# A filter read straight into SBUF by SyncE's queue, and weight conversion steps placed anew, in the opening of a GFNet kernel

## The chip, the cores and the metric

One core of a Trainium2 chip. The metric is the device time of one execution in microseconds (us), the median over runs. PE is TensorE, PEld its weight load, DVE VectorE, ACT ScalarE, POOL GpSimd, SP SyncE; SP computes nothing here and issues transfers.

## The reference

```python
def _attn_ref(x, filt_r, filt_i):            # x: 8 x 3008 x 256, filters: 1505 x 256
    X = np.fft.rfft(x, axis=1)
    F = (filt_r + 1j * filt_i)[None, :, :]
    y = np.fft.irfft(X * F, n=x.shape[1], axis=1)
    return y.astype(np.float32)

def _moe_ref(x, w_in, w_out, alpha=1.0):     # x: 24064 x 256, w_in: 256 x 2048, w_out: 2048 x 256
    h = x @ w_in
    g = np.where(h > 0.0, h, alpha * (np.exp(np.minimum(h, 0.0)) - 1.0))
    return (g @ w_out).astype(np.float32)
```

Each of eight batches of 3008 tokens is mixed along the sequence (real Fourier transform, product with a complex filter, inverse), and the mixed tokens go through a feed-forward layer with an ELU between its two matrices. All is float32, but `moe_w_in` and `moe_w_out` arrive as float64.

## The kernel before

*Mixing.* 3008 = 47 x 64, so the transform is two steps of matmuls with a table of twiddles between (64 points, then 47). The frequencies are done in groups: eight groups g for the first batch. Its inverse goes the same way back, through the DRAM buffers `z` and `yd`.

*Feed-forward.* `w_in` and `w_out` are cut into four quarters q, and each product of two-by-two blocks is done with seven products in place of eight (a Strassen form), which needs sums of blocks of the weights (`w_sums`) and of the data (`n_sums`). An item (b, m, q) is one batch, one sixth of its tokens and one quarter; `up_steps` makes its first matrix product and the ELU, `down_steps` the second. 192 items follow each other; an item's place in this order is called a *quad* (number i). The order of all instructions is written out by hand (`tc.manual_schedule()`, L817), and what belongs to the mixing of the next batch is put into the quads by a dictionary `plan`: `at(quad, place, fn, ...)`, where places 2 and 3 lie within the first half of a quad, 0 in its middle and 1 at its end. Quad i of batch b's mixing counts from t = (b - 1) x 24. The mixing of batch 1 thus runs under the feed-forward of batch 0.

*The opening* (L820 to L936) has the mixing of batch 0, with functions of its own. `x_load_first` reads x in six chunks (SP); `a_first` makes the first transform of a chunk, 16 matmuls, evicted by ACT; `t_first` transposes; `b_first(g)` makes the second transform of a group (PE), then `products` (L336 to L339) multiplies with the filter `ff[:, g]` in four DVE operations of 128 x 512; `bi_first` starts the inverse; `y_write_first` writes it to `yd`. `y_read` and `n_unit` read it back and end the inverse for a sixth m; they are called two quads ahead of the item (m = 0 in the opening).

*The filter* must stand in `ff` with 48 rows for each of two halves (a = 0 in partitions 0 to 47, a = 1 in 64 to 111): 24 even rows, which are frequencies 64 apart counted upwards, and 23 (or 24) odd ones counted downwards. `f_arrange` (L785) first copies both filters into that order in a DRAM tile `fd` (L183), by transfers of POOL's queue whose 23 odd rows go as 16 and 7 (L794); `f_read_first` (L319) then reads a group as one transfer for each half. For batches 1 to 7 `f_pairs` (L804) builds another order `fp` from `fd`, DRAM to DRAM, in four calls (c, u) at the end of quads 1 to 4 in SP's queue; `f_read` reads it with POOL's.

*The weights.* Float64 is made float32 on the chip, in sixteen pieces k of 128 x 512 (four per quarter: two of `w_in`, two of `w_out`). `w_fetch(k)` loads a piece (0.5 MB), `w_split` takes mantissa and exponent bits of the high word (two DVE operations), `w_float` turns low word, mantissa and exponent into floats (four ACT operations), `w_join` sets the sign, adds the mantissa's parts and multiplies by the power of two (three or four DVE operations), `w_sums` makes the block sums of two pieces (four operations). These are spread over the opening and the first quads. Their buffers are borrowed from other work (`fbufs`, `t2`, the x chunks, `zq`, `rq`, ...).

*Queues.* Each engine issues its own transfers in program order. A transfer of SP's queue takes one of eight completion semaphores in turn, so its issue waits until the transfer eight before it has landed. `raw(src, row, ap)` builds an access pattern by hand: a list of [step, count], outermost first.

Of the kernel before, what the change touches and what calls it, by code (L numbers as in the profile page):

```python
# [11 lines left out]
FP32 = mybir.dt.float32  # L12
# [121 lines left out]
def kernel(  # L134
# [48 lines left out]
    fd = fdp.tile([NG, 2, 48, 2, 2, D], FP32, name="fd")  # L183
# [135 lines left out]
    def f_read_first(g, t):  # L319
        for a, r in enumerate((LO, HI)):  # L320
            nc.gpsimd.dma_start(t[r].rearrange("p c u d -> p (c u d)"), fd[g, a].rearrange("q c u d -> q (c u d)"))
# [391 lines left out]
    def w_fetch(k, queue=nc.gpsimd):  # L713
        q, j = divmod(k, 4)

        if k in (3, 4, 14, 15):
            wd = t2[:, k % 11 - 3].rearrange("p u d -> p (u d)")
        elif k == 10:
            wd = t1p.tile([P, XC, D], FP32, tag="t1", name="wd").rearrange("p u d -> p (u d)")
        elif k in (6, 7, 8, 9):  # L720
            wd = xp.tile([P, 2, 2, D], FP32, tag="xc", name="wd").rearrange("p k u d -> p (k u d)")
        else:
            wd = fbufs[{5: 0, 11: 0, 12: 1, 13: 2}.get(k, k)].rearrange("p c u d -> p (c u d)")
        wd = wds[k] = wd.bitcast(U32).rearrange("p (a w) -> p a w", w=2)
        if j < 2:
            srcs = [moe_w_in.bitcast(U32)[ts(j, P), ts(q, 1024)]]
        else:
            srcs = [moe_w_out.bitcast(U32)[ts(4 * q + 2 * (j - 2) + i, P), :] for i in range(2)]
        for i, s in enumerate(srcs):
            n = 512 // len(srcs)  # L730
            queue.dma_start(wd[:, ts(i, n), :].rearrange("p a w -> p (a w)"), s)
# [6 lines left out]
    def w_split(k):  # L738
        m, e, f, l = wts[k] = wtmp[{9: 2, 10: 1, 11: 0, 12: 3, 13: 4, 15: 5}.get(k, k % 2)]
# [4 lines left out]
    def w_float(k, *parts):  # L744
        m, e, f, l = wts[k]
        ef = e.bitcast(FP32)
        steps = ((l, wds[k][:, :, 0], AXT.Identity, 2.0 ** -52, 0.0), (f, m, AXT.Identity, 2.0 ** -20, 1.0),
                 (ef, e, AXT.Relu, -8.0, edges[:, 0:1]), (e, ef, AXT.Relu, -1.0, edges[:, 1:2]))
        for i in parts or range(4):
            o, x, func, scale, bias = steps[i]  # L750
            nc.scalar.activation(out=o, in_=x, func=func, scale=scale, bias=bias)

    def w_join(k, parts=(0, 1)):
        q, j = divmod(k, 4)
        m, e, f, l = wts[k]
        if 0 in parts:
            nc.vector.scalar_tensor_tensor(out=e, in0=wds.pop(k)[:, :, 1], scalar=0x80000000, in1=e,
                                           op0=ALU.bitwise_and, op1=ALU.bitwise_or)
            nc.vector.tensor_tensor(out=f, in0=f, in1=l, op=ALU.add)
        if 1 not in parts:  # L760
            return
        e = e.bitcast(FP32)
        if j < 2:
            f, e = (t.rearrange("p (a j c) -> p a j c", a=2, j=2) for t in (f, e))
            dst = w_in[q][:, 2 * j:2 * j + 2, :, :].rearrange("p j a c -> p a j c")
            nc.vector.tensor_tensor(out=dst, in0=f, in1=e, op=ALU.mult)
        else:
# [3 lines left out]
            for i in range(2):  # L771
                nc.vector.tensor_tensor(out=dst[:, i], in0=f[:, i], in1=e[:, i], op=ALU.mult)
        if j % 2 == 1 and k < 7:
            w_sums(k)
# [10 lines left out]
    def f_arrange():  # L785

        for c, src in enumerate((filt_r, filt_i)):
            for a in range(2):
                nc.gpsimd.dma_start(fd[:, a, 0:48:2, c, :, :].rearrange("g q u d -> q g (u d)"),
                                    raw(src, 2 * a, [[64 * D, 24], [4 * D, NG], [1, 2 * D]]))  # L790
                for u in range(2):
                    g0 = 1 if a == u == 0 else 0
                    for j, n in ((0, 16), (16, 7)):
                        nc.gpsimd.dma_start(fd[g0:NG, a, 1 + 2 * j:2 * (j + n):2, c, u, :].rearrange("g q d -> q g d"),  # L794
                                            raw(src, 64 * (j + 1) - 4 * g0 - 2 * a - u,
                                                [[64 * D, n], [-4 * D, NG - g0], [1, D]]))

                g0 = 0 if a else 1
                nc.gpsimd.dma_start(fd[g0:NG, a, 47, c, :, :].rearrange("g u d -> g (u d)"),
                                    raw(src, 4, [[2 * D, NG - g0], [1, 2 * D]]))  # L800
            nc.gpsimd.dma_start(fd[0, 0, 1:48:2, c, 0, :], raw(src, 32, [[64 * D, 24], [1, D]]))
            nc.gpsimd.dma_start(fd[0, 0, 47:48, c, 1, :], raw(src, 4, [[D, 1], [1, D]]))

    def f_pairs(c, u):  # L804

        src = fd.rearrange("g a q c u d -> (g a) q c u d")[:, :, c, u, :]
        dst = fp.rearrange("g (a u) k c h d -> (g a) u k c h d", u=2)[:, u, :, c, :, :]
        nc.sync.dma_start(dst[:, :, 0, :], src[:, 0:48:2, :])
        g = 1 - u
        nc.sync.dma_start(dst[g:, 1:24, 1, :], src[g:, 1:46:2, :])  # L810
        nc.sync.dma_start(dst[g:, 0, 1, :], nil_d[g:])
        if u == 0:
            nc.sync.dma_start(dst[0, :, 1, :], src[0, 1:48:2, :])

    with tc.manual_schedule():


        with tc.tile_pool(name="boot", bufs=1) as bp:
# [10 lines left out]

            for z in zt[0] + zt[1]:  # L830
                nc.gpsimd.memset(z.rearrange("p (k r) -> p k r", r=ROWS)[:, :, 48:64], 0.0)
            for k in (1, 2, 3):
                w_fetch(k)
            f_arrange()
            w_fetch(0, nc.sync)
            for c in range(NXC):
                x_place_first(c)
            for c in range(3):
                x_load_first(c)
            w_fetch(4, nc.sync)  # L840
            nc.scalar.memzero(ff[:, 0:NG // 2])
            nc.vector.memset(ff[:, NG // 2:NG], 0.0)
            def places(m, e, c):
                wtmp.append((m.bitcast(U32), e.bitcast(U32), c[:, 0], c[:, 1]))

            def flat(t):
                return t.rearrange("p a b -> p (a b)")

            places(*(kp.tile([P, 512], FP32, tag=t, name=n) for t, n in (("k0", "wm"), ("k1", "we"))),
                   kp.tile([P, 2, 512], FP32, tag="c", name="wfl"))  # L850
            places(*(flat(sdp.tile([P, 2, D], FP32, tag="sd", name=n)) for n in ("wm", "we")),
                   t1p.tile([P, XC, D], FP32, tag="t1", name="wfl").rearrange("p (a b) d -> p a (b d)", a=2))
            for i, v in enumerate((1151.0 * 2 ** 23, 255.0 * 2 ** 23)):
                nc.vector.memset(edges[:, i:i + 1], v)

            def step(k):
                w_split(k)
                w_float(k)
                if k > 0:
                    w_join(k - 1)  # L860

            for k in range(3):
                step(k)
            w_fetch(5, nc.sync)
            for c in (3, 4):
                x_load_first(c)
            a_first(0)
            w_fetch(6, nc.sync)
            x_load_first(5)
            nc.sync.dma_start(once, once_d)  # L870
            nc.sync.dma_start(gs, gs_d)
            step(3)
            for c in (1, 2):
                a_first(c)
                w_fetch(c + 6, nc.sync)
            step(4)
            a_first(3)
            w_fetch(9, nc.sync)
            step(5)
            step(6)  # L880
            for c in (4, 5):
                a_first(c)
            tn_read(0, 0)
            for g in range(NG):
                f_read_first(g, ff[:, g])
            w_fetch(10)
            c = t1p.tile([P, XC, D], FP32, tag="t1", name="wfl").rearrange("p (a b) d -> p a (b d)", a=2)
            places(c[:, 0], flat(tnp.tile([P, 4, P], FP32, tag="tn", name="we")), c)
            for t in (zq, rq):
                t = t.rearrange("p a u d -> p a (u d)")  # L890
                places(t[:, 0], t[:, 1], t[:, 2:4])
            t = t3f.rearrange("p a (b u) d -> p (a b) (u d)", u=2)
            places(t[:, 0], t[:, 1], t[:, 2:4])
            w_split(7)
            w_join(6)
            w_split(8)
            floats = {0: (7, 0, 1), 1: (7, 2, 3), 2: (8, 0, 1), 3: (8, 2, 3), 4: (9, 0, 1), 5: (9, 2, 3), 6: (10, 0, 1)}
            for g in range(4):
                t_first(g)
            for g in range(NG + 2):  # L900
# [9 lines left out]
                if g in floats:  # L910
                    w_float(*floats[g])
                if g == 1:
                    w_split(9)
                if g == 2:
                    w_join(7)
                    w_sums(7, nc.gpsimd)
                if g == 5:
                    w_split(10)
                if 3 <= g < 6:
                    w_fetch(g + 8, nc.sync)  # L920
            y_read(0, 0, slice(0, K2 - 4), slice(K2 - 4, K2))
            for k in (14, 15):
                w_fetch(k, nc.sync)
            w_float(10, 2, 3)
            w_join(8)
            for k in (11, 12, 13):
                w_split(k)
                w_float(k)
            w_join(9)
            w_sums(9)  # L930
            w_join(10)
            w_join(11)
# [22 lines left out]
        for quad, place, fn, *a in ((0, 0, w_split, 14), (0, 0, w_sums, 11), (1, 2, w_join, 12), (1, 2, w_split, 15), (1, 2, w_float, 14, 0, 1),  # L955
                                    (1, 3, w_float, 14, 2, 3), (2, 2, w_float, 15, 0, 1), (2, 3, w_float, 15, 2, 3),
# [120 lines left out]
```

## Time and profile before

| what | value |
|---|---|
| median of 3 runs | 2561.13 us (2560.88 to 2561.38) |
| profiled execution, its own time | 2561.57 us |
| its span | 2559.8 us |
| PE busy | 2519.9 us, 98% of the span |
| PEld busy | 2162.6 us, 84% |
| DVE busy | 2067.4 us, 81% |
| ACT busy | 1543.9 us, 60% |
| POOL busy | 159.5 us, 6% |
| SP's queue (q1) | 214308 packets, 166.86 MB |
| POOL's queue (q0) | 14000 packets, 30.44 MB |
| first matmul of the feed-forward (L574) | 88.01 us |

The span is the time from the first to the last instruction that the profiler saw, and the time of the same execution is 1.8 us longer. A share of busy time is an average over the span: the opening and the feed-forward have different limits, and are read apart below. In a chain of waits each row is a piece of the path that ended last: when it starts, how long it takes, and which engine, tile and line it is. In rows by stretch, (x17) is the number of instructions that fell into it, and a DMA share of 1.00 means that all sixteen DMA engines of the core were busy all the time (it can come out a little above).

### The profile page before, as it was taken

Reading aid. Unit: us, or ns where it says so; the run is one execution under the profiler, and the core shown is the slowest. Engines: PE = TensorE matmul, PEld = TensorE weight load, DVE = VectorE, ACT = ScalarE, POOL = GpSimd, SP = SyncE. Lnnn points to the kernel's source line nnn. Section 1 sums busy time; section 2 is a strip of 40 time slices with the busy share of each in tenths; the row PEclk is TensorE's granted clock in tenths of the full one; section 3 lists DMA queues with packets and bytes.
Section 4 is the critical chain, followed back from the end, with each engine's and each line's share of the span. In section 5 each row is a group of like instructions: output and inputs, shape, how many; then the busy total and the mean of one; then the engine's idle time right before and its main releaser. Section 6 shows DMA issues by size and latency. Waiting matters only on the chain.

```text
span 2559.8 us, 43989 instructions
## 1 busy us (share of the span) xinstructions
PE 2519.9 (98%) x16682; PEld 2162.6 (84%) x16682; DVE 2067.4 (81%) x3578; ACT 1543.9 (60%) x2715; POOL 159.5 (6%) x315
## 2 busy tenths in 40 slices
PE   6999999999999999999999999999999999999998
PEld 4788889888898888988889888888889888898887
DVE  6978887788878888688877888778897788876766
ACT  6766556655566555666566656566655655555554
POOL 5001000000000000000000000000100010000000
PEclk9999999999999999999999999999999999999999
DMA  9662213523233221433225231353213322110010
GB/s 282 183 186 67 59 44 78 131 63 71 48 99 98 69 66 40 127 81 74 51 51 143 66 77 36 77 123 80 66 38 84 87 63 63 38 44 18 20 27 17
DMA packets 229879, 200.56 MB, mean 78 GB/s; under 512 B 129398, under 2 KB 201990, under 8 KB 229668
## 3 DMA queue, kind: packets, MB, share of 16 engines
q1 hardware_dynamic: 214308, 166.86, 26.6%
q0 software_dynamic: 14000, 30.44, 4.2%
q8 instruction: 131, 2.15, 0.4%
q14 instruction: 80, 0.66, 0.1%
q10 hardware_dynamic: 1360, 0.46, 0.1%
HBM read 125.80 MB, written 78.12 MB: 80 GB/s over the span
## 4 chain that ended last, share of the span: by engine, by line
PE 96%; DMA 2%; DVE 1%; ACT 0%; issue 0%; SPq 0%; DVEq 0%; ACTq 0%
PE po L656 45%; PE phs L574 25%; PE phd L574 13%; PE pha L574 6%; PE psn L526 2%; PE psa L236 2%; PE pf L387 1%; PE pv L459 1%; DMA xc<-in_x_dram 1%; PE po L332 0%; DMA x<-in_x_dram 0%; PE po L298 0%; PE psr L332 0%; PE psa L279 0%; DVE g L582 0%
## 5 line engine op out<-in xcount | busy, mean ns | idle before, releaser
L656 PE MATMUL po<-g,wo 128*128 128x256 f32 (+1 forms) x5376 | 1317.7, 377 | 0.0
L656 PEld LDWEIGHTS po<-g,wo 128*128 128x128 f32 x5376 | 1010.7, 190 | 165.8 <-issue 49.6
L585 ACT ACTIVATE g<-phs 128x512 f32<-128x512 f32 (+1 forms) x576 | 338.8, 588 | 736.7 <-PE phs L574 735.3
L592 ACT ACTIVATE e<-e 128x512 f32<-128x512 f32 (+1 forms) x768 | 477.2, 621 | 24.4
L596 DVE SCALAR_TENSOR_TENSOR g<-e,g 128x512 f32<-128x512 f32 (+1 forms) x576 | 387.5, 673 | 13.7 <-ACT e L592 13.3
L582 DVE TENSOR_TENSOR g<-phd,g 128x512 f32<-128x512 f32 (+1 forms) x384 | 259.0, 674 | 165.1 <-ACT e L592 107.6
L574 PE MATMUL phs<-y,wi 128*128 128x256 f32 (+1 forms) x1536 | 387.6, 375 | 1.3 <-ACT y L509 1.3
L574 PE MATMUL phd<-y,wi 128*128 128x256 f32 (+1 forms) x1504 | 380.3, 375 | 0.0
L591 ACT ACTIVATE e<-g 128x512 f32<-128x512 f32 (+1 forms) x576 | 354.4, 615 | 34.3 <-DVE g L582 26.8
L574 PEld LDWEIGHTS phs<-y,wi 128*128 128x128 f32 x1536 | 291.4, 190 | 34.7 <-ACT y L509 1.5
L574 PEld LDWEIGHTS phd<-y,wi 128*128 128x128 f32 x1504 | 284.8, 190 | 35.1 <-DVE g L582 2.7
L596 DVE SCALAR_TENSOR_TENSOR g<-e,phs 128x512 f32<-128x512 f32 (+1 forms) x192 | 129.9, 677 | 115.2 <-ACT e L592 115.2
L574 PE MATMUL phs<-yt,wi 128*128 128x256 f32 (+1 forms) x768 | 193.9, 375 | 0.9 <-ACT g L585 0.9
L574 PE MATMUL phs<-yb,wi 128*128 128x256 f32 (+1 forms) x768 | 193.8, 375 | 0.6 <-ACT g L585 0.6
L574 PE MATMUL pha<-yb,wi 128*128 128x256 f32 (+1 forms) x736 | 185.9, 375 | 0.0
L591 ACT ACTIVATE e<-phs 128x512 f32<-128x512 f32 (+1 forms) x192 | 112.3, 585 | 111.9 <-PE phs L574 111.8
L582 DVE TENSOR_TENSOR g<-pha,g 128x512 f32<-128x512 f32 (+1 forms) x192 | 129.5, 674 | 44.8 <-PE pha L574 44.8
L574 PEld LDWEIGHTS phs<-yt,wi 128*128 128x128 f32 x768 | 145.7, 190 | 18.0 <-ACT g L585 1.5
L574 PEld LDWEIGHTS phs<-yb,wi 128*128 128x128 f32 x768 | 144.0, 190 | 19.3 <-ACT g L585 1.0
L326 POOL DMA_DIRECT2D fall<-fp x224 | 110.0, 499 | 721.9 <-DVE r L432 697.1
L574 PEld LDWEIGHTS pha<-yb,wi 128*128 128x128 f32 x736 | 139.8, 190 | 16.1
L633 DVE TENSOR_TENSOR g<-g,g 128x512 f32<-128x512 f32 (+1 forms) x192 | 130.7, 681 | 6.7
(166 smaller groups left out, 2063.3 us busy)
## 6 DMA issues: line engine op xcount, KB each, us to landing
yd<-t SPq DMA_DIRECT2D x127, 192.0 KB
t<-yd SPq DMA_DIRECT2D x92, 256.0 KB
z<-t SPq DMA_DIRECT2D x84, 256.0 KB
fall<-fp POOLq DMA_DIRECT2D x224, 96.0 KB, 2.9
t<-z SPq DMA_DIRECT2D x224, 96.0 KB
out_dram<-o SPq DMA_DIRECT2D x632, 32.0 KB
xc<-in_x_dram SPq DMA_DIRECT2D x84, 128.0 KB
xc<-in_x_dram SPq DMA_DIRECT2D x161, 64.0 KB
```

The lines of the kernel that those rows point to most:

```text
L236: nc.tensor.matmul(p[o:o + 64, u, :], w[r, u, o:o + 64], src[r, u, :], start=True, stop=True)
L326: nc.gpsimd.dma_start(t[32 * a:32 * a + 24].rearrange("p c u d -> p (c u d)"), fp[g, a].rearrange("q c u d -> q (c u d)"))
L387: nc.tensor.matmul(pf[p][1][32 * a:32 * a + 32, js, :], fb[r, v, :], t2[r, js, a, :], start=True, stop=True, tile_position=(32 * p, 32 * a))
L526: nc.tensor.matmul(p[ts(c, 64), dh, ts(q, 64)], t[r, i - 4 * m, ds(dh * P + 64 * c, 64)], w[r, i - 4 * m, :], start=True, stop=True)
L574: nc.tensor.matmul(ps[:, a, 0:h], w_in[q][:, COMBO[n], a, :], y[n], start=start and a == 0, stop=True, skip_group_check=True)
L582: nc.vector.tensor_tensor(out=g[o], in0=i0, in1=i1, op=ALU.add)
L585: nc.scalar.activation(out=g[o], in_=i0, func=AXT.Copy)
L591: nc.scalar.activation(out=e, in_=src, func=AXT.Relu, scale=-1.0)
L592: nc.scalar.activation(out=e, in_=e, func=AXT.Exp, scale=-1.0)
L596: nc.vector.scalar_tensor_tensor(out=g[n], in0=es[n], scalar=1.0, in1=src, op0=ALU.subtract, op1=ALU.max)
L633: nc.vector.tensor_tensor(out=b12, in0=b22, in1=b12, op=ALU.subtract)
L656: nc.tensor.matmul(po[i][:, u, 0:h], w_out[q][:, COMBO[n], a, :], g[n][:, a, :], start=q == 0 and a == 0 and n in (1, 3, 6, 4), stop=True, ...
```

## The change

In the opening the DRAM copy `fd` and `f_arrange` go. `f_read_first(g, n)` reads n groups at once from `filt_r` and `filt_i` into `ff`, by SP's queue: for each filter and half one transfer of the 24 even rows (2 KB runs for each group) and up to two of the 23 odd rows (1 KB runs), 36 transfers in three calls for group 0, groups 1 to 3 and groups 4 to 7. They stand behind the last chunk of x and two tables (`once`, `gs`), ahead of weights 4 to 7, the first inverse's twiddles (`tn_read`) and weight 8. Weights 0 to 2 are loaded by POOL's queue at the start, all others by SP's. `f_pairs` reads the filters themselves; the transfer of the 23 odd rows now has these 23 outermost on both sides (before: the 15 or 16 half-groups).

The conversion: `w_float` has three ACT steps, and a fourth for k > 9; the sign is a function `w_sign`; `w_join` scales and adds the mantissa in one DVE operation for k up to 9, adds on POOL for k > 9, and multiplies on POOL for k from 4; all `w_sums` are on POOL. Splits and floats stand one per group in groups 3 to 7 of the opening (after `products`), and those of pieces 11 to 15 in quads 0 to 2, two pieces each, with sign, join and sums. Buffers of the pieces are assigned anew.

```diff
-    fd = fdp.tile([NG, 2, 48, 2, 2, D], FP32, name="fd")
...
-    def f_read_first(g, t):
-        for a, r in enumerate((LO, HI)):
-            nc.gpsimd.dma_start(t[r].rearrange("p c u d -> p (c u d)"), fd[g, a].rearrange("q c u d -> q (c u d)"))
+    def f_read_first(g, n):
+
+        t = ff[:, g:g + n]
+        for c, src in enumerate((filt_r, filt_i)):
+            for a in range(2):
+                o = 64 * a
+                k = 4 * g + 2 * a
+                nc.sync.dma_start(t[o:o + 48:2, :, c].rearrange("q g u d -> q g (u d)"),
+                                  raw(src, k, [[64 * D, 24], [4 * D, n], [1, 2 * D]]))
+                for u in range(2):
+                    e = 1 if k + u == 0 else 0
+                    if n > e:
+                        nc.sync.dma_start(t[o + 1:o + 47:2, e:n, c, u],
+                                          raw(src, 64 - 4 * e - k - u, [[64 * D, 23], [-4 * D, n - e], [1, D]]))
+            if g == 0:
+                nc.sync.dma_start(t[1:48:2, 0, c, 0], raw(src, 32, [[64 * D, 24], [1, D]]))
...
-    def w_fetch(k, queue=nc.gpsimd):
+    def w_fetch(k, queue=nc.sync):
...
     def w_split(k):
-        m, e, f, l = wts[k] = wtmp[{9: 2, 10: 1, 11: 0, 12: 3, 13: 4, 15: 5}.get(k, k % 2)]
+        m, e = wts[k] = wtmp[k % 3 if k < 10 else (1, 3, 4, 0)[k % 4 - 2]]
...
-    def w_float(k, *parts):
-        m, e, f, l = wts[k]
-        ef = e.bitcast(FP32)
-        steps = ((l, wds[k][:, :, 0], AXT.Identity, 2.0 ** -52, 0.0), (f, m, AXT.Identity, 2.0 ** -20, 1.0),
-                 (ef, e, AXT.Relu, -8.0, edges[:, 0:1]), (e, ef, AXT.Relu, -1.0, edges[:, 1:2]))
+    def w_float(k):
+
+        m, e = wts[k]
+        ef, l = e.bitcast(FP32), wds[k][:, :, 0]
+        steps = [(l.bitcast(FP32), l, AXT.Identity, 2.0 ** -52, 1.0),
+                 (ef, e, AXT.Relu, -8.0, edges[:, 0:1]), (e, ef, AXT.Relu, -1.0, edges[:, 1:2])]
+        if k > 9:
+            steps.append((m.bitcast(FP32), m, AXT.Copy, 2.0 ** -20, 0.0))
...
+    def w_sign(k):
+        m, e = wts[k]
+        nc.vector.scalar_tensor_tensor(out=e, in0=wds[k][:, :, 1], scalar=0x80000000, in1=e,
+                                       op0=ALU.bitwise_and, op1=ALU.bitwise_or)
+
+    def w_join(k):
         q, j = divmod(k, 4)
...
+        e, f, l = e.bitcast(FP32), m.bitcast(FP32), wds.pop(k)[:, :, 0].bitcast(FP32)
+        if k > 9:
+            nc.gpsimd.tensor_tensor(out=f, in0=f, in1=l, op=ALU.add)
+        else:
+            nc.vector.scalar_tensor_tensor(out=f, in0=m, scalar=2.0 ** -20, in1=l, op0=ALU.mult, op1=ALU.add)
+        engine = nc.vector if k < 4 else nc.gpsimd
...
-                nc.vector.tensor_tensor(out=dst[:, i], in0=f[:, i], in1=e[:, i], op=ALU.mult)
-        if j % 2 == 1 and k < 7:
-            w_sums(k)
+                engine.tensor_tensor(out=dst[:, i], in0=f[:, i], in1=e[:, i], op=ALU.mult)
...
-    def f_arrange():
...
     def f_pairs(c, u):
 
-        src = fd.rearrange("g a q c u d -> (g a) q c u d")[:, :, c, u, :]
+        src = (filt_r, filt_i)[c]
         dst = fp.rearrange("g (a u) k c h d -> (g a) u k c h d", u=2)[:, u, :, c, :, :]
-        nc.sync.dma_start(dst[:, :, 0, :], src[:, 0:48:2, :])
+        nc.sync.dma_start(dst[:, :, 0, :], raw(src, u, [[2 * D, 2 * NG], [64 * D, 24], [1, D]]))
         g = 1 - u
-        nc.sync.dma_start(dst[g:, 1:24, 1, :], src[g:, 1:46:2, :])
+        nc.sync.dma_start(dst[g:, 1:24, 1, :].rearrange("g k d -> k g d"),
+                          raw(src, 64 - 2 * g - u, [[64 * D, 23], [-2 * D, 2 * NG - g], [1, D]]))
...
+            for k in range(3):
+                w_fetch(k, nc.gpsimd)
...
+            step(0)
+            a_first(0)
+            w_fetch(3)
+            for c in (4, 5):
                 x_load_first(c)
...
             nc.sync.dma_start(once, once_d)
             nc.sync.dma_start(gs, gs_d)
+            for g, n in ((0, 1), (1, 3), (4, 4)):
+                f_read_first(g, n)
+            step(1)
+            a_first(1)
+            step(2)
+            a_first(2)
+            a_first(3)
             step(3)
...
             for c in (4, 5):
                 a_first(c)
+            for k in range(4, 8):
+                w_fetch(k)
             tn_read(0, 0)
-            for g in range(NG):
-                f_read_first(g, ff[:, g])
...
+            w_fetch(8)
+            w_sign(3)
+            w_join(3)
+            for k in (1, 3):
+                w_sums(k, nc.gpsimd)
...
+                if 3 <= g < 9:
+                    if g < 8:
+                        w_split(g + 1)
+                        w_float(g + 1)
+                    if g > 3:
+                        w_sign(g)
+                        w_join(g)
+                    if g == 7:
+                        for k in (5, 7):
+                            w_sums(k, nc.gpsimd)
+                if 4 <= g < 7:
+                    w_fetch(g + 5)
...
-            for k in (14, 15):
-                w_fetch(k, nc.sync)
...
+            for k in (12, 13, 14, 15):
+                w_fetch(k)
+            w_split(9)
+            w_float(9)
+            w_split(10)
+            w_float(10)
+            w_sign(9)
             w_join(9)
-            w_sums(9)
-            w_join(10)
-            w_join(11)
+            w_sums(9, nc.gpsimd)
...
+        for quad, place, fn, *a in ((0, 2, w_sign, 10), (0, 2, w_join, 10), (0, 2, w_split, 11), (0, 2, w_float, 11),
+                                    (0, 0, w_sign, 11), (0, 0, w_join, 11), (0, 0, w_sums, 11, nc.gpsimd),
+                                    (0, 0, w_split, 12), (0, 0, w_float, 12),
+                                    (1, 2, w_sign, 12), (1, 2, w_join, 12), (1, 2, w_split, 13), (1, 2, w_float, 13),
+                                    (1, 0, w_sign, 13), (1, 0, w_join, 13), (1, 0, w_sums, 13, nc.gpsimd),
+                                    (1, 0, w_split, 14), (1, 0, w_float, 14),
+                                    (2, 2, w_sign, 14), (2, 2, w_join, 14), (2, 2, w_split, 15), (2, 2, w_float, 15),
+                                    (2, 0, w_sign, 15), (2, 0, w_join, 15), (2, 0, w_sums, 15, nc.gpsimd)):
```

## The prediction

> **What bounds the kernel now.** I read the shares by engine first, then the chain of waits, then busy time in 20 us stretches. Chain of the whole span:
>
> ```profile
> PE 96%; DMA 2%; DVE 1%; ACT 0%; issue 0%; SPq 0%; DVEq 0%; ACTq 0%
> ```
>
> PE is full but for the opening, where the chain runs (start, length in us, what):
>
> ```profile
> 15.18 14.30 DMA xc<-in_x_dram
> 29.50 10.89 DMA x<-in_x_dram
> 40.53 3.63 PE psa L279 x16
> 48.28 0.36 PE psr L332
> 67.48 0.26 PE psi L332
> 74.47 0.60 DVE zq L339
> 85.07 1.71 ACT rq L751 x3
> 88.01 1.02 PE phs L574 x4
> ```
>
> So x's last piece lands at 40.39; the eight frequency groups run from 48.3 to 75.1 (PE sets their pace, 2.57 us a group: forward 0.95, back 1.72); then the weights' last steps, and the first FFN matmul at 88.01. Behind it (stretch, length, busy PE, PEld, DVE, ACT, POOL, then PE clock, DMA share, GB/s):
>
> ```profile
> 20.00:40.00 20.00, 12.11 (x64) 11.27 (x64) 9.15 (x20) 11.25 (x26) 8.72 (x16) 0.83 1.05 343
> 40.00:60.00 20.00, 19.01 (x144) 13.38 (x148) 15.52 (x31) 14.95 (x31) 9.56 (x18) 0.91 1.00 285
> 80.00:100.00 20.00, 15.73 (x74) 12.07 (x73) 16.70 (x36) 16.66 (x31) 0.00 (x0) 1.00 0.96 252
> 120.00:140.00 20.00, 19.39 (x144) 16.73 (x143) 18.68 (x36) 14.01 (x25) 0.52 (x1) 1.00 0.60 168
> ```
>
> DMA is saturated to 60 us; PE has gaps up to about 140 us, none later. Whatever the change does is thus seen in the opening, in the first quads, and where a late transfer makes a full PE wait.
>
> **How a transfer is shared out.** The row that decides this forecast is the DMA share while one kind of transfer runs alone: transfers of 16 rows (L810), of 64 (L310), of 24 (L316), of 24 again (L470):
>
> ```profile
> 105.50:106.00 0.50, 0.50 (x5) 0.50 (x4) 0.50 (x3) 0.42 (x1) 0.00 (x0) 1.00 1.07 330
> 157.00:157.75 0.75, 0.75 (x56) 0.75 (x60) 0.00 (x0) 0.60 (x1) 0.75 (x2) 1.00 0.93 290
> 163.75:164.10 0.35, 0.35 (x3) 0.32 (x2) 0.35 (x2) 0.35 (x1) 0.00 (x0) 1.00 0.76 199
> 219.50:222.00 2.50, 2.50 (x14) 2.19 (x13) 2.40 (x7) 0.60 (x1) 0.00 (x0) 1.00 0.70 143
> ```
>
> 16 and 64 rows fill the 16 engines, 24 rows keep 0.70 to 0.76 of them: 12, each with two rows. I read it as equal shares: as many engines as the largest number up to 16 that divides the outermost rows. The change makes transfers whose outermost dimension is 23 rows, a prime: one engine. Before has none: the 23 odd rows of a filter half are split 16 + 7 (L794), and the copy into pairs (L810) has 15 or 16 outermost. Price of a 1 KB row on one engine: 330 GB/s over 16 engines is 20.6 GB/s, 50 ns; 290 over 0.93 x 16 is 52 ns; 255 over 0.93 x 16 (0 to 20 us) 60 ns; 143 over 0.70 x 16 80 ns. I take 50, from the row with the same 1 KB runs; ends 46 (the median 1 KB packet of the trace) and 80.
>
> The Trainium skill, "DMA: Bandwidth & Descriptors", section "Why a DMA increments its semaphore by 16 and not by 1", states the same: the largest k up to 16 dividing the slowest dimension on both sides, with 127 partitions as an example of k = 1. The trace agrees at 24 rows; no run here shows a prime yet. It speaks against this change: by it 23 rows have a sixteenth of the bandwidth.
>
> **Part by part.**
>
> *x.* Ahead of x5 the old order has the copy into DRAM and weights 4 to 6, written and read (GpSimd's issues from 4.6 to 35.5 us). Now about 6.8 MB stand there (x, its tables, weights 0 to 3): at (255+343)/2 = 299 GB/s 22.8 us, plus some 2.5 to start: 25 instead of 40.4. The first group could then start at 34.5, not 48.3: 14 us gained.
>
> *Filter straight into SBUF.* Odd rows by size: group 0 6 x 23 = 138 KB, groups 1 to 3 8 x 69 = 552, 4 to 7 8 x 92 = 736; 1426 rows of 1 KB. The even ones (24 rows, 2 KB runs, 1.57 MB on 12 engines) put another 128 on the same engine. 1554 x 50 ns = 78 us, the first just before x's end: last landing near 102.5. Group 0 is there at 32, 1 to 3 at 62, 4 to 7 at 102. Transfers with few engines don't run at once either: each of SyncE's waits for its eighth predecessor, and they queue on the same engine anyhow.
>
> *What waits for it.* Weights 4 to 7, the twiddles of the first inverse and weight 8 stand behind all 36 in SyncE's queue: weight 4 at 103.6. On VectorE the split of weight 4 stands ahead of the products of group 4: these start at 104.3 (before: 49.4 + 4 x 2.57 + waits, near 64). Behind products 4 each group has on VectorE products 4 x 0.60 = 2.4, split 2 x 0.335, sign 0.6, join 0.65: 4.3 us, and thrice this and the last 2.4 is 15.3; the sign waits some 2 to 3 us for ScalarE's three float steps (0.57 each behind two evictions of 0.5 that come later): last product at about 122.5, 47.4 later than 75.07. From there to the first FFN matmul 12.94 us before; now weights 9 and 10 only (two splits, floats, one sign, join and four sums of 0.76 on GpSimd), and the last group's evictions, y's write and read: I keep 13. First FFN matmul 135.6: **+47.6 us**. What x gained lies wholly under it.
>
> *Weights' last steps.* One ScalarE step and an add fewer for weights 4 to 9: hidden under the wait. For 11 to 15 whole sets (four ScalarE steps, 0.57 x 4 = 2.3 us) now stand in quads 0 to 2, two per quad, where before six float steps and joins were spread over quads 1 to 3. PE in quads 0 to 3 now needs 48.8 us for 4, some 41 at a full clock without gaps; ScalarE is busy 16.7 of 20 us at 80 to 100. Ten sets of splits and floats less what was there add 9 to 10 us of ScalarE work to about 50 us where 10 of 60 were free, and each float waits for a split queued behind the previous quad's last VectorE operations: three gaps of 3 to 4 us. **+10 us**; ends 0 (all into the free share) and +14. Sums on GpSimd: 0.76 against 0.68 in the one pair of rows (L783), off the path until sums 15.
>
> *Pairs read from the filter.* Same 23 outermost: 345 + 368 + 345 + 368 = 1426 rows, 71 us on one engine, issued at the places of quads 1 to 4, from about 150 on: third set served near 218, fourth 248. In SyncE's queue y's read for the third item (L489) stands behind the third set: landing near 220, while PE has nothing more from 211: 13 us. z's read (L316) behind the fourth lands near 258 against 255: 3 to 4 us. **+17 us**; ends 0 (hidden) and, at 80 ns, near +60.
>
> *Gone:* 8.6 us of GpSimd issues and the copy's traffic, both counted under x.
>
> **Sum.** The profiled execution took 2561.57 us (span 2559.8 and 1.8 around it), 0.4 above the median 2561.13, which is nothing here. 2561.6 + 47.6 + 10 + 17 = 2636. Both one-engine terms scale with the row: about 3 us for each ns. 46 ns gives 2624, 60 ns 2666, 80 ns 2726.
>
> **Rivals.**
>
> 1. *Rows are dealt out over all engines, prime or not.* For: 24 rows as two rows on eight engines and one on eight others also have a mean share of 0.75. Against: that would show 1.0 and then 0.5, and the share stays level, also over four in a row. Then the filter lands at about 39, under a_first and the transposes, and x's 14 us reach the first group. Given back: 4.3 - 2.6 = 1.7 us a group for five groups, VectorE-bound (-8), and the 10 in the quads; less 1 for the direct reads: 2561.6 - 14 + 8.5 + 10 - 1.5 = 2564 or so.
>
> 2. *Other side: faster, because the row rule is no limit and the floats lie in ScalarE's free share.* Same dealing as in 1, and the quads' +10 falls to 0 to 2, as ScalarE and VectorE have 3 to 5 us free in each 20. It decides as soon as the quads cost under 5 us. 2561.6 - 14 + 8.5 - 1.5 = 2554. Against: the level share, and 18.68 of 20 us VectorE in 120 to 140.
>
> 3. *One engine in the opening alone.* The pairs' reads are not waited for, as y's read goes ahead on the other engines and needs only a twelfth of its data from the slow one: 2619. Against: all of a transfer must land, and engine 0's part stands behind the queue.
>
> 4. *The change doesn't do what it says:* a group's products wait for all 36 transfers rather than their own; groups 1 to 3 then start at 102 too, PE makes up seven groups at 4.3: 8 more, 2644. Inside the range.
>
> **How the numbers follow.** One engine for 23 rows, forecast 2636: chance 0.89, with rival 3 and 4 in it; its own range 2605 to 2710. Rival 1: 0.07, rival 2: 0.04. Below 0.2% (5.1 us) a measurement of this kernel can't tell a difference from none: rival 1 is within it or just above (0.05 and 0.02), rival 2 faster. Slower 0.91, same 0.05, faster 0.04. The range 2597 to 2710 leaves out the two rivals and rows beyond about 74 ns.
>
> **What would show it.** DMA share near 1/16 from about 40 to 100 us at some 20 GB/s; products of groups 1 and 4 waiting on the filter's transfer and on weight 4's; first FFN matmul near 135; pairs landing 17 us and more after their issue instead of 2; PE idle about 13 us before the third item's inverse. Wrong if the filter lands before 45 us: then the row rule fell. If the wait is there but PE's later gap isn't, rival 3; if quads 0 to 3 take under 52 us, the ScalarE term fell.

## The result and the profile after

The changed kernel takes 2649.5 us (median of 4, 2646.66 to 2651.79) against 2561.26 us (median of 4, 2560.88 to 2562.44): 1.0339 times as long, 95% interval 1.0326 to 1.0352. The profiled execution took 2646.66 us, its span is 2643.7.

Where the 84 us between the two profiled spans arise is read from one VectorE operation that each quad has once near its end (its start, L632 before, L644 after; us from the span's start):

| mark | before | after | later by | since the row above |
|---|---|---|---|---|
| first FFN matmul | 88.01 | 131.93 | 43.9 | 43.9 |
| end of quad 3 | 135.04 | 198.27 | 63.2 | 19.3 |
| end of quad 4 | 148.73 | 211.88 | 63.1 | -0.1 |
| end of quad 6 | 175.20 | 245.70 | 70.5 | 7.4 |
| end of quad 8 | 202.85 | 286.94 | 84.1 | 13.6 |
| end of quad 191 | 2545.02 | 2628.96 | 83.9 | -0.2 |

Four places, then, and nothing behind 290 us. The chain of the whole span, of the kernel after:

```profile
PE 92%; SPq 3%; DMA 2%; DVE 1%; ACT 1%; issue 0%; DVEq 0%; ACTq 0%
```

SyncE's queue (SPq), 0% before, now holds 3% of 2644 us, 84 us. The chain through the opening (start, length, what):

```profile
19.02 8.68 DMA x<-in_x_dram
...
69.54 4.34 SPq L325
73.92 0.64 SPq L330
74.61 3.84 SPq L330
...
83.22 3.97 SPq L330
87.30 4.25 SPq L745
91.65 8.90 DMA wd<-in_moe_w_in_dram
```

x ends at 27.7 instead of 40.4. From there to 87.2 the chain lies in SyncE issuing the filter's transfers, in groups 4 to 7 an even one and two of 92 rows in 8.0 to 9.0 us; then it issues weight 4 (L745 at 87.30), and the chain's last row is weight 5, for which SyncE's writes of `yd` wait. The same time by stretches (columns as before):

```profile
40.00:60.00 20.00, 5.89 (x43) 3.17 (x41) 0.69 (x1) 3.33 (x6) 0.00 (x0) 0.70 0.14 46
80.00:100.00 20.00, 0.00 (x0) 0.00 (x0) 0.71 (x3) 0.68 (x1) 0.00 (x0) 0.50 0.47 150
```

DMA share 0.14 at 46 GB/s where before it was 1.00 at 285: the odd rows hold one engine, the even rows a little of twelve. The trace also has the times at which a transfer's completion semaphore is raised, and I read one raise for each engine at work. A weight (128 rows) raises it sixteen times. A transfer of 24 rows raises it once 0.4 us after its issue and then twelve times, which fits its share of 0.70 to 0.76; one of 23 rows raises it once after its issue and then a single time (issued at 43.63: 46.86 and 55.15). The last odd rows land at 98.1, and of weight 4's sixteen raises fifteen come by 95.3 and the last at 99.26: one engine still had the filter's rows ahead of it. VectorE's instructions in that time (start, length, what, and in brackets the idle time before and what ended it):

```profile
48.76 0.69 DVE L348 TENSOR_TENSOR rq<-psr,ff 128x512 f32<-128x512 f32 x1 [8.96 <-DMA ff<-in_filt_r_dram]
62.18 0.69 DVE L349 TENSOR_TENSOR rq<-psr,ff 128x512 f32<-128x512 f32 x1 [12.73 <-DMA ff<-in_filt_i_dram]
99.29 0.43 DVE L755 TENSOR_SCALAR wme<-wd 128x512 uint32<-128x512 uint32 x1 [28.14 <-DMA wd<-in_moe_w_in_dram]
```

Group 1 waits for the real, then for the imaginary filter until 62.2; group 4 stands behind weight 4's split at 99.3.

The late losses, from SyncE's own queue:

```profile
198.67 0.59 SPq L807 DMA_DIRECT2D fp<-in_filt_i_dram  x1
199.31 0.66 SPq L809 DMA_DIRECT2D fp<-in_filt_i_dram  x1
200.01 11.69 SPq L811 DMA_DIRECT2D fp<-nil_t  x1
211.75 0.76 SPq L813 DMA_DIRECT2D fp<-in_filt_i_dram  x1
```

L809 is the transfer with 23 rows outermost (345 or 368 runs of 1 KB). It is issued in 0.66 us, but the small transfer behind it (L811, 15 or 16 KB) takes 11.7 us to issue. It doesn't wait for the transfer eight before it, which had landed at 198.3. In all four calls this issue ends 5.3 to 5.4 us before the transfer with 23 rows lands (211.70 and 217.06 here), which I read as SyncE standing in the issue until the one engine's queue has room; the trace gives the times, not the reason. Everything in its program order is that much later; in the chain L309's write of z and ScalarE's eviction that waits for its buffer follow, then PE.

### The profile page after: what moved, and what is told of

The parts are those of the page before. It is cut to its first block, busy times and chain, and to the rows that moved or that the text cites. A ratio compares the mean times of both kernels' runs of the same rounds, so it can differ in the third digit from the quotient of the medians.

```text
span 2643.7 us, 43983 instructions
## 1 busy us (share of the span) xinstructions
PE 2543.0 (96%) x16682; PEld 2173.6 (82%) x16682; DVE 2059.9 (78%) x3526; ACT 1538.6 (58%) x2705; POOL 182.0 (7%) x320
## 4 chain that ended last, share of the span: by engine, by line
PE 92%; SPq 3%; DMA 2%; DVE 1%; ACT 1%; issue 0%; DVEq 0%; ACTq 0%
PE po L668 43%; PE phs L586 24%; PE phd L586 12%; PE pha L586 6%; PE psn L538 2%; PE pf L399 1%; PE psa L235 1%; PE pv L471 1%; SPq L330 1%; SPq L325 1%; DMA xc<-in_x_dram 1%; SPq L811 0%; DMA z<-t 0%; DMA yd<-t 0%; DMA wd<-in_moe_w_in_dram 0%; DMA x<-in_x_dram 0%
## 5 line engine op out<-in xcount | busy, mean ns | idle before, releaser
L586 PEld LDWEIGHTS phd<-y,wi 128*128 128x128 f32 x1504 | 286.6, 191 | 35.5 <-DVE g L594 2.6
```

What stands on the lines that cost most here:

```text
L586: nc.tensor.matmul(ps[:, a, 0:h], w_in[q][:, COMBO[n], a, :], y[n], start=start and a == 0, stop=True, skip_group_check=True)
```

## The experiments

Ratios are against the kernel before, run beside them.

**Cutting the 23 rows into 16 and 7.** In the opening alone (e1), in the pairs alone (e2), in both (e3), and the reverse in the kernel before (e4).

```diff
 e1:
-                        nc.sync.dma_start(t[o + 1:o + 47:2, e:n, c, u],
-                                          raw(src, 64 - 4 * e - k - u, [[64 * D, 23], [-4 * D, n - e], [1, D]]))
+                        for j, w in ((0, 16), (16, 7)):
+                            nc.sync.dma_start(t[o + 1 + 2 * j:o + 1 + 2 * (j + w) - 1:2, e:n, c, u],
+                                              raw(src, 64 * (j + 1) - 4 * e - k - u, [[64 * D, w], [-4 * D, n - e], [1, D]]))
 e2:
-        nc.sync.dma_start(dst[g:, 1:24, 1, :].rearrange("g k d -> k g d"),
-                          raw(src, 64 - 2 * g - u, [[64 * D, 23], [-2 * D, 2 * NG - g], [1, D]]))
+        for j, w in ((0, 16), (16, 7)):
+            nc.sync.dma_start(dst[g:, 1 + j:1 + j + w, 1, :].rearrange("g k d -> k g d"),
+                              raw(src, 64 * (j + 1) - 2 * g - u, [[64 * D, w], [-2 * D, 2 * NG - g], [1, D]]))
 e4, in the kernel before:
-        nc.sync.dma_start(dst[g:, 1:24, 1, :], src[g:, 1:46:2, :])
+        nc.sync.dma_start(dst[g:, 1:24, 1, :].rearrange("g k d -> k g d"), src[g:, 1:46:2, :].rearrange("g k d -> k g d"))
```

> The changed kernel with the 23 odd rows of each direct filter transfer cut into 16 and 7; nothing else. If 23 outermost rows lie on one DMA engine: the filter is there by 45 us instead of about 91, first FFN matmul 80 to 90 us instead of 131.9, total near 2602 (the 44 us of the opening gone, the later 40 kept). Rival, that the direct reads cost by their number of issues, their 1 KB runs or their place in SyncE's queue: no gain, or 16 more issues of 0.6 us, 2647 to 2657.

Measured: 2620.29 us, 1.0232 (1.0217 to 1.0247); first FFN matmul 108.3. 24 of the opening's 44 us go, not 44. Both theories hold a part. SyncE's rows of e1, the filter of one part (16 or 7 rows, four transfers a row):

```profile
53.78 2.94 SPq L331 DMA_DIRECT2D ff<-in_filt_r_dram  x4
56.76 0.81 SPq L325 DMA_DIRECT2D ff<-in_filt_r_dram  x1
57.62 3.74 SPq L331 DMA_DIRECT2D ff<-in_filt_r_dram  x4
```

Issue follows issue with hardly a wait, mostly 0.6 to 0.8 us each: 58 of them from 22.4 to 69.5, 22 more than in the changed kernel, since each cut makes two of one. Meanwhile the DMA engines are little more than a quarter busy:

```profile
40.00:68.00 28.00, 19.53 (x128) 10.08 (x128) 8.56 (x14) 5.53 (x10) 0.00 (x0) 0.76 0.29 85
```

With the single engine gone, the issues of one queue look like the bound; the run with two queues below tests that.

> The changed kernel with the 23 outermost rows of each of the four pair transfers cut into 16 and 7; nothing else. If these lie on one engine: the losses at quads 5 and 7 (7.4 and 13.6 us) go, total near 2626. Rival, that reading the strided filter in place of the DRAM copy is what costs there: no change, 2647.

Measured: 2628.57 us, 1.0264 (1.0249 to 1.0279), 20.9 below the changed kernel. The issue behind the 23 rows takes 0.52 to 0.84 us instead of 11.4 to 14.6, and from quad 3 to quad 191 nothing more is lost. Reading the strided filter in place of the copy costs nothing here.

> Both cuts together. If the single engine is the whole of both losses: before plus the 19 us of quads 0 to 3, plus or minus what x's earlier end and the new weight steps make of the opening, 2570 to 2585. If those 19 us too came from the cold opening rather than from the weights' steps: 2555 to 2567. Rival (issues and runs): 2640 or more.

Measured: 2601.48 us, 1.0153 (1.0136 to 1.0170): outside both of the theory's ranges, below the rival's. First FFN matmul at 107.4, quads 0 to 3 still 20.9 us longer than before, nothing later.

> The kernel before, with the same DRAM copy as the source of the pairs, but with the 23 rows outermost in place of the 15 or 16 half-groups; nothing else. If 23 outermost rows lie on one engine: SyncE is held for some 17 us at each of the four and PE waits in the first eight quads, 5 to 21 us slower, 2566 to 2582. If the order of the dimensions doesn't matter: 2561.

Measured: 2593.07 us, 1.0125 (1.0110 to 1.0140), 32 us slower and so above the expected 2566 to 2582, where the same four transfers cost 21 in the changed kernel; that they meet quads here which nothing else has made late may be the reason, and wasn't tried. Its queue:

```profile
100.16 0.69 SPq L810 DMA_DIRECT2D fp<-fd  x1
100.90 13.20 SPq L811 DMA_DIRECT2D fp<-nil_t  x1
...
115.76 0.64 SPq L810 DMA_DIRECT2D fp<-fd  x1
116.45 14.42 SPq L811 DMA_DIRECT2D fp<-nil_t  x1
```

Same bytes, same source, same runs of 1 KB, only the dimension that stands outermost: that alone holds SyncE. The first of these transfers raises its semaphore sixteen times in the kernel before, here twice (101.22 and 119.32).

**The odd rows by GpSimd's queue** (e5, on e3): `nc.gpsimd.dma_start` in place of `nc.sync.dma_start` for the cut transfers, which are 44 (the expectation counts 40).

> The kernel with both cuts (2601), its 40 transfers of odd rows issued by GpSimd's queue in place of SyncE's; the even ones stay. There 60 issues of 0.65 to 0.8 us each fill SyncE's queue from 22 to 70 us while the DMA engines are a quarter busy. If the issue rate of one queue is what is left of the opening's loss: filter there by 45 to 50 us, first FFN matmul 83 to 92 in place of 107, total 2580 to 2587. Rival, that the small runs or their landing are slow whoever issues them: 2601.

Measured: 2579.23 us, 1.0072 (1.0057 to 1.0087); first FFN matmul 87.9, as in the kernel before (88.0), the last odd rows landed at 50.6. The last 20 us of the opening's loss were SyncE's issues in one row behind x. The run doesn't part two things: a second queue issues beside the first, and it begins at 6.0 us, where in SyncE's queue these transfers stood behind all of x (22.4).

**Quads 0 to 3.** On e3: the weights' arithmetic of GpSimd back on VectorE (e6), ScalarE's steps one place behind the splits they wait for (e7; with them the signs, joins and sums of weights 11, 13 and 15 go one place later too), and both (e11).

```diff
 e6: w_join's add and multiply and every w_sums: nc.gpsimd -> nc.vector
 e7:
-... (0, 2, w_split, 11), (0, 2, w_float, 11), ... (0, 0, w_split, 12), (0, 0, w_float, 12), ...
+... (0, 2, w_split, 11), (0, 0, w_float, 11), ... (0, 0, w_split, 12), (0, 1, w_float, 12), ...
```

> The kernel with both cuts (2601), with every weight multiply, add and sum that the change put on GpSimd back on VectorE. In the changed kernel VectorE's integer and scalar_tensor_tensor operations take 0.94 and 1.22 us in place of 0.42 and 0.68 while GpSimd computes. If this slowing is what makes quads 0 to 3 20 us longer: 2585 to 2595. Rival, that VectorE has no room for some 20 us more work there: 2601 to 2615.

> The kernel with both cuts (2601), with the ScalarE steps of weights 11 to 15 one place later than VectorE's splits that they wait for; same work, no engine changed. If ScalarE stands on the splits while PE waits for its evictions: 8 to 12 us of the 20 in quads 0 to 3 go, 2589 to 2593. Rival, that it is the amount of work: 2599 to 2602.

> The kernel with both cuts, the weights' arithmetic on VectorE and the ScalarE steps one place later than their splits, together (both cuts alone 2601, VectorE alone 2605, later steps alone 2595). If, once ScalarE no longer stands on the splits, GpSimd's slowing of VectorE is what is left: 2588 to 2592, quads 0 to 3 some 8 us longer than in the kernel before instead of 14. Rival, that VectorE has no room: 2597 to 2605.

Measured: e6 2605.34 us, 1.0173 (1.0156 to 1.0190); e7 2595.19, 1.0138 (1.0123 to 1.0153); e11 2596.56, 1.0131 (1.0118 to 1.0145). e6 falls to its rival, e7 gives 6 where 8 to 12 were expected, e11 nothing beyond e7 (just below its rival's range). In e6 quads 0 to 3 are as long as in e3, and the 4 us more are in the opening (first FFN matmul at 111.6 instead of 107.4). What e7 takes away is seen in ScalarE's rows of the kernel after, in brackets its idle time before:

```profile
138.29 1.48 ACT L767 ACTIVATE rq<-rq,edges 128x512 f32<-128x512 uint32 x2 [3.51 <-DVE rq L756]
155.99 1.48 ACT L767 ACTIVATE we<-we,edges 128x512 f32<-128x512 uint32 x2 [4.48 <-DVE we L756]
174.54 1.48 ACT L767 ACTIVATE rq<-rq,edges 128x512 f32<-128x512 uint32 x2 [3.23 <-DVE rq L756]
```

Three waits for a split, 11.2 us in all; in e7 ScalarE has none, and 6 us come back. Busy time from the first FFN matmul to the end of quad 3, added up from the instructions that start in it (overlaps counted once, so to within some 0.5 us):

| kernel | length | VectorE weights / rest | ScalarE weights | GpSimd weights |
|---|---|---|---|---|
| before | 47.0 | 13.3 / 30.1 | 4.8 | 0 |
| after | 66.3 | 14.3 / 34.9 | 12.4 | 29.4 |
| e3 | 67.9 | 14.3 / 35.5 | 12.5 | 29.5 |
| e6 | 67.7 | 20.1 / 30.1 | 12.7 | 0 |
| e7 | 61.3 | 12.5 / 36.0 | 12.2 | 29.5 |
| e11 | 59.1 | 19.8 / 30.0 | 12.2 | 0 |
| e12 | 58.8 | 9.1 / 34.7 | 9.7 | 28.5 |

GpSimd takes 5.8 us of weight work from VectorE (e6 less e3), and beside it VectorE's other work takes 5.4 us longer. The two are about equal, and undoing the move changes nothing in quads 0 to 3. The slowing itself, VectorE and GpSimd side by side in the kernel after, first without, then with GpSimd at work:

```profile
117.20 0.42 DVE L755 TENSOR_SCALAR wm<-wd 128x512 uint32<-128x512 uint32 x1
117.88 0.67 DVE L771 SCALAR_TENSOR_TENSOR wme<-wd,wme 128x512 uint32<-128x512 uint32 x1
...
123.30 0.94 DVE L755 TENSOR_SCALAR wme<-fall 128x512 uint32<-128x512 uint32 x1
125.04 1.22 DVE L771 SCALAR_TENSOR_TENSOR we<-fall,we 128x512 uint32<-128x512 uint32 x1
```

```profile
121.06 3.78 POOL L801 TENSOR_TENSOR wi<-wi 128x256 f32<-128x256 f32 x4
124.80 2.04 POOL L801 TENSOR_TENSOR wo<-wo 128x256 f32<-128x256 f32 x2
```

0.42 becomes 0.94, 0.67 becomes 1.22, and GpSimd's own sum 0.94 instead of the 0.76 that it took before. The buffer isn't the reason: in e6, without GpSimd's work, the same two operations on `fall` take 0.42 and 0.69. The Trainium skill, "GPSIMD Engine Reference", section "8. Key points", says that GpSimd shares its SBUF interfaces with VectorE instructions that have two SBUF inputs or run in a two-port mode. The trace agrees for the operation with two inputs (0.67 to 1.22); in which mode the one with a single input (0.42 to 0.94) ran, no row shows.

**The direct read in the kernel before.** The copy `fd` gone, weights as before, filter by GpSimd's queue where the copy was issued: with 16 and 7 rows (e8), with 23 (e9), and e8 with groups 4 to 7 held to about 25 us (e10: VectorE's clearing of that half of `ff`, and `f_read_first(4, 4)`, behind the third weight's steps). Pairs cut as in e2.

> The kernel before with one part of the change: the copy in DRAM gone, the filter read directly into SBUF by GpSimd's queue at the place of the copy, with 16 and 7 rows, and the pairs read from the filters with 16 and 7 rows; weights as before. If the direct read is worth what its smaller traffic says: x's last piece lands 8 to 15 us earlier, total 2546 to 2553. Rival, that the weights' steps on VectorE and ScalarE set the opening's end in any case: 2558 to 2562.

> The kernel before with the direct read by GpSimd's queue (2561.9), its odd rows as 23 uncut; the pairs keep 16 and 7. If 23 rows lie on one DMA engine whichever queue issues them: the last group's filter some 70 us after the first, near 80 us instead of 60, products of groups 4 to 7 wait, 2580 to 2595. Rival, that GpSimd's queue deals rows out in another way: 2560 to 2563, with 16 issues fewer at most 5 us less.

> The kernel before with the direct read by GpSimd's queue (2561.9), with groups 4 to 7 held until VectorE has cleared their half of the tile, which now stands behind the third weight's steps (near 25 us). If x is late there because the filter's 1 KB rows share the DMA engines with it: x's last piece 3 to 6 us before 39.4, total 2555 to 2559. Rival, that the weights' steps set the opening's end: 2561 to 2564.

Measured: e8 2561.89 us, 1.0003 (0.9994 to 1.0013); e9 2569.94, 1.0029 (1.0017 to 1.0041); e10 2564.17, 1.0007 (0.9999 to 1.0016). e8 comes out at its rival's time and e10 at the end of its rival's range, but the reason that the traces show is another: in e8 x ends at 39.4, only 1 us earlier, and in e10 at 43.5, later, so that the weights' steps were not put to the test. The stretch from 20 to 40 us of e8, then two of e9:

```profile
20.00:40.00 20.00, 10.07 (x52) 9.14 (x52) 11.16 (x24) 11.71 (x26) 11.18 (x20) 0.70 1.08 236
```

```profile
20.00:40.00 20.00, 8.40 (x40) 7.94 (x40) 7.48 (x15) 8.21 (x19) 11.28 (x11) 0.75 1.11 232
40.00:60.00 20.00, 16.23 (x114) 12.79 (x115) 13.54 (x26) 13.43 (x28) 8.99 (x9) 0.74 1.09 182
```

All DMA engines are busy as before, but at 236 GB/s instead of 343: one copy of the filter fewer, and the engines no freer. e9 is between its two expectations, 8 us and not some 18 to 33 slower than before: 23 rows from GpSimd's queue keep the DMA engines full (1.09 to 1.11), where the same rows from SyncE's leave 0.14. So they don't all lie on one engine there. Whether each transfer is spread, or each takes another engine, these rows don't tell, but the raises of the semaphores speak for the second: of the first uncut transfer with three groups (issued at 19.63) fifteen come from 28.91 to 29.63 and the last at 33.18, 3.8 us behind the middle one, where with 16 and 7 rows (e8) the last is at most 0.5 us behind for the transfers of that time. An issue with three or four groups takes 1.25 us in place of some 0.55.

The Trainium skill, "DMA: Bandwidth & Descriptors", section "Why a DMA increments its semaphore by 16 and not by 1", has both: SyncE's queue takes the lowest-numbered engines, GpSimd's moves on from one transfer to the next, or spreads some copies over all sixteen. The trace agrees with the difference between the queues; the one late raise speaks for one engine, and then another, rather than for a spread over all sixteen.

**All together** (e12, on e5): of the weights' steps 11's split and float, 10's sign and join in the opening's tail; 12 to 15 over quads 0 to 3, ScalarE's steps a place behind the splits, last sums in quad 3.

> The kernel with both cuts and the odd rows on GpSimd's queue (2579), with the steps of weights 11 to 15 placed anew: split and float of 11, sign and join of 10 in the opening's tail; of 12 to 15 one piece a quad or fewer, each ScalarE step a place after its split, the last sums in quad 3. If where the steps stand is all that makes quads 0 to 3 longer: the 20 us fall to 4 or less, 2561 to 2566, level with the kernel before. Rival, that the pieces' work itself costs there whatever its place: 2570 to 2574, as the later ScalarE steps alone would give.

Measured: 2570.29 us, 1.0033 (1.0021 to 1.0046), the rival's time. Quads 0 to 3 are still 11.8 us longer than before. No version here is shown to beat the kernel before.

## Why the prediction was right, step by step

It forecast 2636 (2597 to 2710), slower with 0.91; measured 2649.5. The mechanism it rested on, that a row count of 23 outermost lies on one DMA engine in SyncE's queue, is shown by the two raises of the semaphore, by e4 and e2, and by e1 for the opening. Term by term, in the profiled execution:

- *Row price* 50 ns: on one engine one filter's half for groups 4 to 7 takes 8.8 us (chain: L325 at 60.86, 69.54, 78.49) for 184 odd rows and the engine's 16 KB of the even ones: 200, 44 ns each. Below the lower bound of 46.
- *x's end* 25, measured 27.7. *Groups 1 to 3* at 62, measured 62.2. *The filter's last landing* at 102.5, measured 98.1, *weight 4* at 103.6, measured 99.3, *last product* 122.5 against 117.3, *the tail* 13 against 14.6: **opening +47.6, measured +43.9**. That what waits at group 4 is weight 4's split was right.
- But why the odd rows cost 44 us was half seen. The prediction let transfers queue on the engine and gave the issue no price; its first rival had the filter at 39 and 2564 us in all if rows were spread. With spread rows (e3) it is 2601 and the filter's last rows land at 72.5: **the failed step is that a spread filter would lie hidden under x**, as in e1, with the same cut, 58 issues hold SyncE for 47 us. (22 of these issues are the cut's own; rows spread without a cut were not run.) Before, GpSimd issued its copy from 4.6 us on, beside SyncE.
- *Quads 0 to 3* **+10, bounds 0 and +14; measured +19.3, outside.** ScalarE's extra work was sized well (9 to 10; 7.6 measured), and so were the three gaps of 3 to 4 us (3.51, 4.48, 3.23). The step that failed is that nothing was put beside the gaps: without them (e7) quads 0 to 3 are still 14.3 us longer than before. VectorE, 43.7 of 47 us busy before, got more pieces' splits, signs and joins there, and what moved to GpSimd came back as slower VectorE operations. Sums on GpSimd were called off the path and not priced for that; their 0.76 was set against 0.68, but VectorE's rows of L783 in the kernel before take 0.42.
- *Pairs* **+17; measured 20.9**, but the place was wrong: not y's read waiting its turn on the engine, with 13 us at the third item, but SyncE held in the issue behind each 23-row transfer, 7.4 us by quad 6 and 13.6 more by quad 8.

So two terms were too small by 9 and 4, one too large by 4: 75 worked out, 84 measured in the profiled spans. That the sum came this near is in part luck: the quads' term lay outside its own bounds, the pairs' wait was another than the one described, and the opening's 4 us went the other way.

The rivals: 1 and 2 fall with the two raises and with e1 to e4; 3 falls with e2 (the pairs cost 21); 4 doesn't hold, since group 0's products ran at 37.3 and groups 1 to 3 from 62.2.

What stays open: of the 19 to 21 us in quads 0 to 3, 6 go with the later places (e7), which I put down to ScalarE's waits for the splits. The other 12 to 14 remained in each of three placements (e7, e11, e12). VectorE's fullness is argued from its busy time, not shown by a run that takes the pieces out of the quads. About half of the rest is not PE waiting but PE being slower: in e12 it is busy 49.5 of 58.8 us with 257 matmuls, in the kernel before 43.2 of 47.0 with 256, at a mean granted clock of 0.87 against 1.00. Of the 11.8 us, 6.3 are thus longer matmuls, by their modelled ends, and 5.5 idle time. In the kernel after the clock was granted at 0.71 to 0.90 in the first three quads. That the gaps bring the lower clock was not tried by itself.

## What to carry to other kernels

Put a dimension outermost whose size is a multiple of 16, or at least of a large number below it, and look at the DMA share of the stretch in which a new transfer runs alone: 0.14 beside a waiting engine is a shape, not bandwidth. Count issues by queue as well as bytes: two queues side by side, the second beginning 16 us earlier, were worth 22 us here with no byte changed. Before work is moved to an idle engine, look at what it shares with the one it relieves, and at how full the engine is at the new place rather than on average.

## What the runs showed that was not expected

- An issue can block: behind a transfer of 345 or 368 rows on one engine SyncE's next issue took 11.4 to 14.6 us (four in the changed kernel, 0.52 to 0.84 with the rows cut), though it moves only 15 or 16 KB itself.
- The same 23 rows keep the DMA engines full from GpSimd's queue (1.09 to 1.11) and nearly idle from SyncE's (0.14).
- The direct read saved a copy of the filter and not the engines' time: from 20 to 40 us 236 GB/s at a share of 1.08, against 343 at 1.05 with the copy.
- Three waits of ScalarE, 11.2 us together, were worth only 6 us when they were gone, and PE ran at a mean granted clock of 0.85 to 0.89 in these quads in the changed kernel and in e3, e6, e7, e11 and e12, against 1.00 in the kernel before.
